# Pair sums in the plain pair, early w2 groups, merged steps and own residual buffers in a token-mixing kernel

## The chip, the cores and the metric

The kernel runs on one core of a Trainium2 chip. The metric is device time in microseconds (us) of one execution. The core has five engines that run beside each other and wait for one another through semaphores: TensorE (PE in the profile; its weight loads stand as PEld), VectorE (DVE), ScalarE (ACT), GpSimd (POOL) and SyncE (SP), which here only issues DMAs. Every engine, and the DMA queue that an engine feeds, works through its own instructions in order.

## The reference

A linear attention block is followed by a token-mixing MLP, all in fp32, for S = 2048 tokens, D = 512 channels and F = 1792 hidden rows:

```
h  = x + A(layernorm(x))                 # linear attention, wqkv, w_phi, wo
n  = layernorm(layernorm(h))             # one from the outer block, one inside the MLP
u  = gelu(einsum("bsd,sf->bdf", n, w1) + b1)
y  = einsum("bdf,fs->bds", u, w2) + b2
out = h + transpose(y)                   # (S, D)
```

The change touches only the MLP: the product with w1 (over the 2048 tokens), the gelu, the product with w2 (over the 1792 hidden rows) and the last addition.

## The kernel before

**Numbers.** An fp32 operand is split into a high part rounded to fp32r and the rest (`split`, line 59: ACT copies the high part, another engine subtracts). A product of two operands is three fp32r matmuls: high by high, high by low, low by high (`mm3`).

**Attention.** It fills the first half of the time and leaves h in `out` and the normalised tokens `HN[t]` (16 tiles of 128 tokens, high and low) in the buffers of the pool `big`. The change does not touch it.

**w1.** The 14 tiles of 128 hidden rows are worked on in seven pairs p = 0 to 6. Pairs 0, 1, 2 and 6 are plain: 16 token tiles by 2 row tiles by 3 matmuls of 512 columns. Pairs 3, 4 and 5 (`SEVEN`) use a scheme with seven products in place of eight on 2 by 2 blocks: a step takes two token tiles, and has 7 products by 3 matmuls of 256 columns, 21 in all (`seven_step`, line 933). The loop over `RUN` counts n = 0 to 29: n = 0 to 5 are the last six steps of plain pair 2, n = 6 to 13 pair 3, n = 14 to 21 pair 4, n = 22 to 29 pair 5. Pair 6 (`fill`, the lines L66 to L68) comes after the loop, with its weights streamed by `stream` (L670 load, L671 high part, L665 low part).

For each step of `RUN` the weights pass through rings of tiles: SP loads a raw tile (`seven_load`, L868, 4 deep), DVE forms the sums that the seven products need (`seven_sum`, L888 and L890), ACT makes the high part (L894, 3 deep), and DVE the low part (`seven_lo`, L912, 3 deep). In iteration n the low part of step n+1 and the sums of step n+3 are written down. The DVE's work is thus in one fixed row: low part, sums, and between them whatever else the loop puts there. What it puts there: `seven_out(p-1)` from i = 1 on, two operations for each n (L950 to L956, the recombination of the previous pair's PSUM banks and its gelu), and the operands of the two "near" pairs 0 and 1.

**Operands of w2.** After the gelu each pair's `U[p]` needs three sums in a tile `tt` (lines 807 to 810 or 824 to 827), and each of the seven operands its high and low part. For the near pairs 0 and 1, `near_ops` puts four subtractions on POOL (L807 to L810), two copies on ACT (L816, L817) and two subtractions on DVE (L818, L819); it is called at i = 2 of pair 3 (n = 8) and of pair 4 (n = 16), and the ACT and DVE parts follow at i = 4, 5 and 7. Both use the one buffer `tt` of the pool `ut`. The other five pairs go through `operands_u` (L824 to L827 and L62), whose results lie in buffers of `big` that pair 6 has finished reading; there the odd pairs have their `tt` in the buffer `h7`.

**w2.** The weights come in 28 groups of two steps (`GRP` = 2): a load of 512 KB on SP (`load_w2`, L1048), three sums on DVE (L854 to L856, through `sums_of`), the high part on ACT (`hi_w2`, L1066), the low part on DVE (`lo_w2`, L1076). The loads of groups 0, 1 and 2 go to the buffers `hold0` to `hold2`, in which the w1 stage keeps the transformed tokens of i = 0, 1 and 2. `STEPS` is 8 pairs of output tiles sp by 7 pairs p. A step (`step`) is seven products: five wide ones, each with a 512-column matmul by the high weights and a 256-column one by the low weights, and two narrow ones of three 256-column matmuls. For p = 0, and for the last two p (three in the last sp), `products` goes product by product, and for the others `step` does all wide matmuls by the high weights, then those by the low ones, then the narrow ones. At an even step count the next group's low part, the second next one's high part and the third next one's sums are written down.

**The end.** For the first seven sp the results go out through a tile `ot` (pool `uo`, one buffer) with accumulating DMAs on POOL's queue. In the last sp the residual h is loaded from `out` (L1185) into the two halves of the same kind of tile, b2 is added (L1186), then the PSUM banks are added in on DVE as their products end (L1188 to L1198), and SP and ACT issue the last stores.

**What sets the order.** Inside a `manual_schedule` block the named engines keep the order in which the code writes their instructions. What stands outside, such as pair 6's fills, `operands_u` and all of SP's loads, is placed by a planner that simulates the time line and may put it between the instructions of such a block. The first three w2 groups are placed by it too, with `issue_after` as a lower bound.

## Time and profile before

| | |
|---|---|
| median of 3 runs | 521.54 us (521.18 to 522.02) |
| profiled execution | 521.74 us, span 520.0 us |
| PE busy | 511.8 us, 98% of the span |
| DVE busy | 445.0 us, 86% |
| ACT, POOL busy | 296.6 us (57%), 245.7 us (47%) |
| granted TensorE clock | 1.000 |

The span runs from the first to the last instruction; about 1.7 us of the execution's time lie around it. "Busy" for PE counts a matmul from its start to a modelled end, and neighbours overlap, so a short wait of PE can hide in a row that looks fully busy; the distance between the starts of two matmuls tells more. In rows of the time line the first number is the start in us from the span's begin, the second the time to the end of the last instruction of the row, then come engine, line of the kernel, operation, tiles (out<-in), shapes and count, and in brackets the idle time of the engine just before, with what ended it.

### The profile page before, as it was taken

How to read it: one execution, taken by the hardware profiler on the slowest of the kernel's cores; microseconds unless marked ns; L12 is line 12 of the kernel's file. 1: busy time of each engine (PE TensorE's matmuls, PEld its weight loads, DVE VectorE, ACT ScalarE, POOL GpSimd, SP SyncE). 2: the span in 40 equal slices, each digit the busy share in tenths (PEclk: the TensorE clock that was granted, in tenths of full speed). 3: DMA queues.
4: the chain of work that ended last, by engine and by line, in shares of the span. 5: the costliest groups of instructions: out<-in, count | busy, mean ns of one | idle time of the engine just before them, and what ended most of it. 6: DMA issues, size and time to landing. Idle time of an engine off the chain costs nothing. (4 is left out here: it accounts for less than half of the span.)

```text
span 520.0 us, 9480 instructions
## 1 busy us (share of the span) xinstructions
PE 511.8 (98%) x3595; PEld 442.1 (85%) x3595; DVE 445.0 (86%) x789; ACT 296.6 (57%) x494; POOL 245.7 (47%) x188
## 2 busy tenths in 40 slices
PE   8999999999999999999999999999999999999996
PEld 8788888887877767887788999998889999999996
DVE  6893999986899998877787679998999888988984
ACT  6998943524246876668976443556654434434430
POOL 2589799885999999875533003000002112211220
PEclk9999999999999999999999999999999999999999
DMA  8744310000131234343413333346125688667653
GB/s 310 271 139 122 82 42 21 1 1 3 42 123 60 103 84 129 112 128 119 151 50 101 97 88 102 87 123 236 62 88 112 165 184 171 139 151 190 139 71 102
DMA packets 36300, 58.56 MB, mean 113 GB/s; under 512 B 3744, under 2 KB 19360, under 8 KB 36256
## 3 DMA queue, kind: packets, MB, share of 16 engines
q1 hardware_dynamic: 31648, 50.85, 30.6%
q0 software_dynamic: 4032, 6.42, 9.8%
q8 instruction: 28, 0.46, 0.4%
q10 hardware_dynamic: 576, 0.69, 0.4%
q14 instruction: 16, 0.13, 0.1%
HBM read 46.81 MB, written 11.14 MB: 111 GB/s over the span
## 5 line engine op out<-in xcount | busy, mean ns | idle before, releaser
L1066 ACT ACTIVATE whi<-wraw 128x1792 fp32r<-128x1792 f32 x28 | 47.6, 1701 | 42.5 <-DVE wraw L856 21.1
L1076 DVE TENSOR_TENSOR wlo<-wraw,whi 128x1792 fp32r<-128x1792 f32 x28 | 56.6, 2020 | 8.8 <-PE py L1108 7.5
L1169 POOL DMA_DIRECT2D out<-ot x7 | 6.2, 885 | 110.4 <-DVE ot L1165 110.4
L67 PE MATMUL pu<-hs,whi 128*128 128x512 f32 x128 | 50.3, 393 | 1.2 <-POOL hs L62 1.2
L1104 PE MATMUL py<-uf,whi 128*128 128x512 f32 x175 | 50.0, 395 | 0.4 <-DVE uf L62 0.4
L66 PE MATMUL pu<-hs,whi 128*128 128x512 f32 x128 | 50.1, 399 | 0.0
L68 PE MATMUL pu<-hs,wlo 128*128 128x512 f32 x128 | 48.3, 390 | 0.0
L894 ACT ACTIVATE whi<-wraw 128x896 fp32r<-128x896 f32 x24 | 22.9, 953 | 33.8 <-DVE wraw L890 18.6
L456 POOL TENSOR_TENSOR ez<-eq,zB 128x1024 f32<-128x1024 f32 x16 | 38.4, 2400 | 4.4 <-ACT zB L503 4.4
L1108 PE MATMUL py<-uf,whi 128*128 128x256 f32 x210 | 39.0, 283 | 0.0
L933 PE MATMUL pu<-ht,whi 128*128 128x256 f32 x192 | 35.6, 283 | 0.0
L208 POOL TENSOR_TENSOR pk<-pk,sk 128x1024 f32<-128x1024 f32 x16 | 30.9, 1940 | 7.3 <-DVE sk L207 7.2
L62 POOL TENSOR_TENSOR hs<-hb,hs 128x512 fp32r<-128x512 f32 x16 | 22.4, 1400 | 23.9 <-ACT hs L61 23.8
L550 ACT ACTIVATE pht<-tn 128x512 f32<-128x512 f32 x32 | 17.4, 595 | 28.4 <-PE tn L548 28.3
L474 POOL TENSOR_TENSOR eq<-eq,w 128x1024 f32<-128x1024 f32 x16 | 32.4, 2027 | 1.3 <-DVE w L471 1.2
L1108 PEld LDWEIGHTS py<-uf,whi 128*128 128x128 f32 x210 | 32.7, 192 | 0.0
L1104 PEld LDWEIGHTS py<-uf,wlo 128*128 128x128 f32 x175 | 28.5, 189 | 4.9
L1104 PEld LDWEIGHTS py<-uf,whi 128*128 128x128 f32 x175 | 29.2, 189 | 3.4 <-DVE uf L62 0.7
L212 POOL TENSOR_TENSOR zacc<-zacc,pk 128x1024 f32<-128x1024 f32 x13 | 31.3, 2405 | 0.5
L66 PEld LDWEIGHTS pu<-hs,whi 128*128 128x128 f32 x128 | 24.0, 188 | 7.1 <-issue 2.5
L933 PEld LDWEIGHTS pu<-ht,whi 128*128 128x128 f32 x192 | 29.9, 192 | 0.0
L912 DVE TENSOR_TENSOR wlo<-wraw,whi 128x896 fp32r<-128x896 f32 x24 | 26.0, 1085 | 4.5 <-ACT whi L894 4.5
(207 smaller groups left out, 1626.9 us busy)
## 6 DMA issues: line engine op xcount, KB each, us to landing
wraw<-in_w SPq DMA_DIRECT2D x28, 512.0 KB, 4.5
wraw<-in_w SPq DMA_DIRECT2D x48, 256.0 KB, 2.8
xraw<-in_xT SPq DMA_DIRECT2D x16, 256.0 KB, 3.1
xh<-in_x SPq DMA_DIRECT2D x16, 256.0 KB, 2.7
h<-in_x SPq DMA_DIRECT2D x16, 256.0 KB, 2.7
out<-h SPq DMA_DIRECT2D x14, 256.0 KB, 2.9
out<-ot POOLq DMA_DIRECT2D x14, 256.0 KB, 4.9
wraw<-in_wT SPq DMA_DIRECT2D x12, 256.0 KB, 4.9
```

Source lines behind the costliest of these rows:

```text
L66: nc.tensor.matmul(o, ah, bh, start=first, stop=False)
L67: nc.tensor.matmul(o, ah, bl, start=False, stop=False)
L68: nc.tensor.matmul(o, al, bh, start=False, stop=last)
L208: nc.gpsimd.tensor_mul(heads(PK[t]), heads(PK[t]), sk.unsqueeze(2).to_broadcast([P, 2 * H, DH]))
L212: nc.gpsimd.tensor_add(zacc, zacc, PK[t])
L456: nc.gpsimd.tensor_mul(EZ[t], EQ[t], zB)
L474: nc.gpsimd.tensor_mul(heads(EQ[t]), heads(EQ[t]), W[t].rearrange("p g c h -> p (g c h)").unsqueeze(2).to_broadcast([P, 2 * H, DH]))
L933: nc.tensor.matmul(ACC[p][bk][:, half], WS[p, i][x][:, a], hb[b][y], start=i == 0 and half == 0 and k == 0, stop=i == NT // 2 - 1 and k == ...
L1066: nc.scalar.activation(WH[g], RAW[g], AF.Copy)
L1076: nc.vector.tensor_sub(wl_, RAW[g], WH[g])
L1104: nc.tensor.matmul(o, w, u, start=p == 0 and not low, stop=p == NP - 1, skip_group_check=True)
L1108: nc.tensor.matmul(bank[bk][:, half], AW[sp, p][x][:, a], UB[p, b][:, y], start=p == 0 and half == 0 and i == 0, stop=p == NP - 1 and i == ...
```

## The change

Five things are done.

1. `near_ops` is called at n = 1 (pair 0) and n = 4 (pair 1), within plain pair 2, and its ACT and DVE parts follow at n = 2, 3, 4 and n = 6, 8, 10. The `tt` of pair 1 goes to the buffer `h7` (`sums_tile`).
2. The helpers for w2's groups stand ahead of the loop. Groups 0 and 1 are loaded at n = 23 and 24 (pair 5, i = 1 and 2), their sums are written at n = 27 and 28, the high part of group 0 at n = 27. The high part of group 1, the low part of group 0 and load and sums of group 2 follow `seven_out` of pair 5, inside the block with written order.
3. In the w2 stage two steps of one group that both go through `step` are merged (`steps`): the wide matmuls by the high weights of both, and then for each of them the rest.
4. In the last sp the residual goes to two buffers of its own, `hb0` and `hb1`.
5. The tile `raw3` is taken for group 4, the first that uses that place, where the code before asked for group 3 and so allocated the place once more.

```diff
--- before.py
+++ after.py
@@ -800,10 +800,13 @@
         nc.scalar.activation(U[f // 2][:, f % 2 * 2:f % 2 * 2 + 2].rearrange("p k d -> p (k d)"), pu,
                              AF.Gelu_apprx_tanh, bias=b1s[:, f:f + 1])
 
+    def sums_tile(p):
+        return h7.tile([P, 3, HD], F32, name="tt", tag="h7") if p % 2 else ut.tile([P, 3, HD], F32, name="tt")
+
     def near_ops(p):
 
         u = U[p]
-        tt = ut.tile([P, 3, HD], F32, name="tt")
+        tt = sums_tile(p)
         nc.gpsimd.tensor_sub(tt[:, 0], u[:, 0], u[:, 1])
         nc.gpsimd.tensor_sub(u[:, 0], u[:, 2], u[:, 0])
         nc.gpsimd.tensor_sub(tt[:, 1], u[:, 2], tt[:, 0])
@@ -820,7 +823,7 @@
 
     def operands_u(p):
         u = U[p]
-        tt = h7.tile([P, 3, HD], F32, name="tt", tag="h7") if p % 2 else ut.tile([P, 3, HD], F32, name="tt")
+        tt = sums_tile(p)
         nc.vector.tensor_sub(tt[:, 0], u[:, 0], u[:, 1])
         nc.vector.tensor_sub(u[:, 0], u[:, 2], u[:, 0])
         nc.vector.tensor_sub(tt[:, 1], u[:, 2], tt[:, 0])
@@ -955,6 +958,51 @@
                 lambda: nc.vector.tensor_add(u[:, 2], acc[2][:, 1], u[:, 2]),
                 lambda: act(1) or nc.vector.tensor_add(u[:, 0], acc[1][:, 1], u[:, 0]) and act(0)]
 
+    STEPS = [(sp, p) for sp in range(NT // 2) for p in range(NP)]
+    NGR = len(STEPS) // GRP
+    RAW, WH, AW = {}, {}, {}
+    done = {"sums": 0, "hi": 0, "lo": 0}
+
+    def load_w2(g):
+        slot = g % 3 if g < 4 else (3, 1, 2, 0)[g % 4]
+        shape = [P, 7, GRP * P]
+        if slot == 3:
+            RAW[g] = raw3 if g == 4 else hp.tile(shape, F32, name="wraw3", bufs=1)
+        else:
+            RAW[g] = hold(shape, F32, "wraw", slot)
+        nc.sync.dma_start(RAW[g][:, 1:5], w2[g])
+
+    def sums_w2():
+
+        g = done["sums"]
+        if g == NGR:
+            return
+        done["sums"] += 1
+        if g not in RAW:
+            load_w2(g)
+        sums_of(RAW[g])
+
+    def hi_w2():
+
+        g = done["hi"]
+        if g == NGR:
+            return
+        done["hi"] += 1
+        WH[g] = keep([P, 7, GRP * P], F32R, "whi", g % 3)
+        nc.scalar.activation(WH[g], RAW[g], AF.Copy)
+
+    def lo_w2():
+
+        g = done["lo"]
+        if g == NGR:
+            return
+        done["lo"] += 1
+        shape = [P, 7, GRP * P]
+        wl_ = hp.tile(shape, F32R, name="wlo1", bufs=1) if g % 2 else keep(shape, F32R, "wlo", 3)
+        nc.vector.tensor_sub(wl_, RAW[g], WH[g])
+        for i, step in enumerate(STEPS[g * GRP:(g + 1) * GRP]):
+            AW[step] = WH[g][:, :, i * P:(i + 1) * P], wl_[:, :, i * P:(i + 1) * P]
+
     six, seven = ([lambda i=i, k=k: t_sums(i, k) for k in range(4)] for i in (6, 7))
     t_hi(4)
     for op in six[:2]:
@@ -976,7 +1024,8 @@
         return [lambda c=c: gelu(2 * p + c, PU[p][c]) for c in range(2)]
 
     early = {0: [*seven, *gelus(0)], 1: [lambda: t_lo(6), lambda: t_hi(7), *gelus(1)], 3: [lambda: t_lo(7)]}
-    todo, heavy, late = [], [], []
+    todo, late = [], []
+    NEAR_AT, LATE_AT = (1, 4), (2, 3, 4, 6, 8, 10)
     for n, (p, i) in enumerate(RUN):
         if n == NT // 2 - AHEAD:
             ms.close()
@@ -991,17 +1040,19 @@
                 op()
         sum_with(*todo[:2])
         todo = todo[2:]
-        if heavy:
-            op = heavy.pop(0)
-            op and op()
         if i == 1 and p > SEVEN[0]:
             todo += seven_out(p - 1)
-        if i == 2 and 0 <= p - SEVEN[0] < NEAR:
-            late = near_ops(p - SEVEN[0])
-        if i == 4 and late:
+        if n in NEAR_AT:
+            late += near_ops(NEAR_AT.index(n))
+        if late and n in LATE_AT:
             late.pop(0)()
-            heavy += [late[0], None, late[1]]
-            late = []
+        at = n - len(RUN)
+        if -7 <= at < -5:
+            load_w2(at + 7)
+        if -3 <= at < -1:
+            sums_w2()
+            if at == -3:
+                hi_w2()
     wst.close()
     hp = ctx.enter_context(tc.tile_pool(name="hp", bufs=1, reuse_waits="tile"))
     wst = ExitStack()
@@ -1020,6 +1071,9 @@
     flush()
     for op in seven_out(SEVEN[-1]):
         op()
+    hi_w2()
+    lo_w2()
+    sums_w2()
     ms.close()
     while FN[NP - 1] < NT:
         if FN[NP - 1] % 2 == 0:
@@ -1033,58 +1087,6 @@
     wst.close()
     uo = ctx.enter_context(tc.tile_pool(name="uo", bufs=2, reuse_waits="tile"))
 
-    STEPS = [(sp, p) for sp in range(NT // 2) for p in range(NP)]
-    NGR = len(STEPS) // GRP
-    RAW, WH, AW = {}, {}, {}
-    done = {"sums": 0, "hi": 0, "lo": 0}
-
-    def load_w2(g):
-        slot = g % 3 if g < 4 else (3, 1, 2, 0)[g % 4]
-        shape = [P, 7, GRP * P]
-        if slot == 3:
-            RAW[g] = raw3 if g == 3 else hp.tile(shape, F32, name="wraw3", bufs=1)
-        else:
-            RAW[g] = hold(shape, F32, "wraw", slot)
-        nc.sync.dma_start(RAW[g][:, 1:5], w2[g])
-
-    def sums_w2():
-
-        g = done["sums"]
-        if g == NGR:
-            return
-        done["sums"] += 1
-        load_w2(g)
-        sums_of(RAW[g])
-
-    def hi_w2():
-
-        g = done["hi"]
-        if g == NGR:
-            return
-        done["hi"] += 1
-        WH[g] = keep([P, 7, GRP * P], F32R, "whi", g % 3)
-        nc.scalar.activation(WH[g], RAW[g], AF.Copy)
-
-    def lo_w2():
-
-        g = done["lo"]
-        if g == NGR:
-            return
-        done["lo"] += 1
-        shape = [P, 7, GRP * P]
-        wl_ = hp.tile(shape, F32R, name="wlo1", bufs=1) if g % 2 else keep(shape, F32R, "wlo", 3)
-        nc.vector.tensor_sub(wl_, RAW[g], WH[g])
-        for i, step in enumerate(STEPS[g * GRP:(g + 1) * GRP]):
-            AW[step] = WH[g][:, :, i * P:(i + 1) * P], wl_[:, :, i * P:(i + 1) * P]
-
-    for i in range(3):
-        with tc.issue_after(LO[-9]), tc.issue_after(LD[(-6, -5, -4)[i]]):
-            sums_w2()
-            if i < 2:
-                hi_w2()
-            if i < 1:
-                lo_w2()
-
     PROD = ((2, 1, 0, None), (5, 5, 1, None), (0, 0, 2, 0), (1, 4, 2, 1), (3, 6, 3, None), (6, 2, 4, None),
             (4, 3, 5, None))
 
@@ -1108,14 +1110,18 @@
             nc.tensor.matmul(bank[bk][:, half], AW[sp, p][x][:, a], UB[p, b][:, y], start=p == 0 and half == 0 and i == 0,
                              stop=p == NP - 1 and i == 2, skip_group_check=True)
 
-    def step(sp, p, order):
-        for low in range(2):
+    def steps(sp, ps, order):
+        for p in ps:
             for a, b, bk, half in order:
                 if half is None:
-                    wide(sp, p, a, b, bk, low)
-        for a, b, bk, half in order:
-            if half is not None:
-                narrow(sp, p, a, b, bk, half)
+                    wide(sp, p, a, b, bk, 0)
+        for p in ps:
+            for a, b, bk, half in order:
+                if half is None:
+                    wide(sp, p, a, b, bk, 1)
+            for a, b, bk, half in order:
+                if half is not None:
+                    narrow(sp, p, a, b, bk, half)
 
     def flat(a):
         return a.rearrange("p k d -> p (k d)")
@@ -1141,7 +1147,8 @@
             products(sp, [p], order)
             continue
         if p < NP - run_on:
-            step(sp, p, order)
+            if n % GRP == 0 or p == 1:
+                steps(sp, range(p, min(p + GRP - n % GRP, NP - run_on)), order)
             continue
         if p < NP - 1:
             continue
@@ -1179,8 +1186,7 @@
                 sums_w2()
             continue
 
-        ot = uo.tile([P, 2, 2, HD], F32, name="ot", bufs=1)
-        hb = [ot[:, i] for i in range(2)]
+        hb = [uo.tile([P, 2, HD], F32, name=f"hb{i}", bufs=1) for i in range(2)]
         for i in range(2):
             nc.sync.dma_start(flat(hb[i]), out[(t + i) * P:(t + i + 1) * P, :])
             nc.vector.tensor_scalar(hb[i], hb[i], b2s[:, t + i:t + i + 1], None, op0=ALU.add)
```

## The prediction

> **What bounds the kernel now.** I read the page first, then the waits of PE and its weight loads, then the busy times by stretch, and last the time line at each place where PE loses time.
>
> ```profile
> span 520.0 us, 9480 instructions
> PE 511.8 (98%) x3595; PEld 442.1 (85%) x3595; DVE 445.0 (86%) x789; ACT 296.6 (57%) x494; POOL 245.7 (47%) x188
> ```
> ```profile
> PEld pu L933 <- DVE wlo L912: 1.3, 4, 0.5
> ```
> PE bounds the kernel, and the change removes no matmul. So it can win only waits of PE, and the time after PE's last matmul. In the stages that it touches, PE waits four times in the loop over the seven-product pairs (L933), and once in the w2 stage, which part 2 shows. Here are the four, to be read by the distances between starts:
>
> ```profile
> 329.63 0.40 PE L933 MATMUL pu<-hs,whi 128*128 128x256 f32 x2
> ...
> 329.99 0.40 PE L933 MATMUL pu<-hs,whi 128*128 128x256 f32 x2
> ...
> 330.84 0.41 PE L933 MATMUL pu<-ht,whi 128*128 128x256 f32 x2
> ```
> ```profile
> 332.99 0.40 PE L933 MATMUL pu<-hs,whi 128*128 128x256 f32 x2
> ...
> 333.58 0.28 PE L933 MATMUL pu<-ht,whi 128*128 128x256 f32 x1
> ```
> ```profile
> 335.74 0.40 PE L933 MATMUL pu<-hs,whi 128*128 128x256 f32 x2
> ...
> 336.65 0.28 PE L933 MATMUL pu<-ht,whi 128*128 128x256 f32 x1
> ```
> ```profile
> 338.80 0.40 PE L933 MATMUL pu<-hs,whi 128*128 128x256 f32 x2
> ...
> 339.40 0.28 PE L933 MATMUL pu<-ht,whi 128*128 128x256 f32 x1
> ```
> Three undisturbed matmuls take 0.36 us (329.63 to 329.99). The four disturbed threes take 0.85, 0.59, 0.91 and 0.60, so 0.49 + 0.23 + 0.55 + 0.24 = 1.51 us are lost. Each time PE waits for the low part of the weights, made by DVE. Busy time by stretch (PE, PEld, DVE, ACT, POOL) shows why:
>
> ```profile
> 280.00:290.00 10.00, 10.00 (x46) 8.29 (x45) 6.28 (x13) 4.02 (x7) 1.33 (x2) 1.00 0.27 80
> ```
> ```profile
> 312.00:333.00 21.00, 20.78 (x174) 20.57 (x173) 20.74 (x42) 10.27 (x13) 4.68 (x4) 1.00 0.36 101
> 333.00:354.00 21.00, 20.71 (x169) 20.15 (x168) 18.82 (x42) 10.22 (x15) 0.00 (x0) 1.00 0.46 138
> 354.00:380.00 26.00, 26.00 (x124) 21.67 (x123) 25.68 (x52) 16.89 (x28) 0.00 (x0) 1.00 0.39 132
> ```
> In pair 4 (312 to 333) DVE is busy for 20.74 of 21 us: here it falls behind. In the plain pair (280 to 290) it has 3.7 of 10 us free, and ACT 6.0.
>
> **Part 1: the near pairs' sums move into the plain pair.** What stands in DVE's row in pair 4 and goes:
>
> ```profile
> 313.85 0.96 DVE L888 TENSOR_TENSOR wraw<-wraw 128x256 f32<-128x256 f32 x1
> 314.84 1.46 DVE L890 TENSOR_TENSOR wraw<-wraw 128x128 f32<-128x128 f32 x2
> ...
> 317.23 0.96 DVE L888 TENSOR_TENSOR wraw<-wraw 128x256 f32<-128x256 f32 x1
> 318.22 0.62 DVE L890 TENSOR_TENSOR wraw<-wraw 128x128 f32<-128x128 f32 x2
> ...
> 319.76 0.42 DVE L888 TENSOR_TENSOR wraw<-wraw 128x256 f32<-128x256 f32 x1
> ```
> ```profile
> 328.34 1.22 DVE L818 TENSOR_TENSOR un<-u,un 128x1024 fp32r<-128x1024 f32 x1
> ...
> 334.42 0.95 DVE L819 TENSOR_TENSOR un<-tt,un 128x768 fp32r<-128x768 f32 x1
> ```
> While POOL does pair 1's four subtractions (its 4.68 us, x4, in the stretch 312 to 333), DVE's sums are stretched: L888 twice from 0.42 to 0.96, L890 once from 0.62 to 1.46, together 1.92 us. L818 takes 1.22 more, right ahead of the first wait at 330. So DVE gets 3.1 us before 330.62, and 0.95 (L819) after that. PE was held up by 0.55 at most at one place, so I count all four waits as gone: **-1.51 us**. Bounds: if the planner fills the freed time with the sums of pairs 2 and 3 ahead of the low parts, the gain is 0; more than 1.51 isn't there. I take 1.51, since the relief is several times the largest wait.
>
> The Trainium skill says in "SBUF — State Buffer", section "Who interferes with whom", that a VectorE instruction with two SBUF inputs and a GpSimd one that reads SBUF exclude each other for a whole instruction. The trace agrees in kind, not in size: 4.68 us of POOL cost DVE 1.92. By the rule DVE could lose all 4.68 wherever these subtractions stand; then the relief here is larger, the gain the same 1.51, and the new place is dearer (rival 4).
>
> At the new place everything issued counts: four POOL subtractions, two ACT copies, two DVE subtractions for each pair. POOL has nothing else there (1.33 us of 10), so nothing queues behind them. ACT's copies come behind the high part of step n+3. DVE's first subtraction (n = 3) waits for ACT's first copy, and the low part of step 5 queues behind it. DVE then has 1.22 + 0.95 for pair 0 and again up to 1.92 of stretching for pair 1, 4.1 us against the 3.7 free in these 10 us, and the code keeps the low parts a step ahead of PE: cost 0; 0.4 without that step, 4.1 without the free time too. Pair 1's two DVE subtractions (n = 8, 10) fall in pair 3, where pair 0's stood, so nothing changes there. `h7` is free once `t_lo(7)` (n = 3) has read it.
>
> **Part 2: w2's first two groups.** From DVE's row, w1's last low part, and later a w2 group's low part, the first of its sums, and pair 6's last operands:
>
> ```profile
> 348.97 1.07 DVE L912 TENSOR_TENSOR wlo<-wraw,whi 128x896 fp32r<-128x896 f32 x1
> ...
> 386.63 2.02 DVE L1076 TENSOR_TENSOR wlo<-wraw,whi 128x1792 fp32r<-128x1792 f32 x1
> 388.56 0.68 DVE L854 TENSOR_TENSOR wraw<-wraw 128x512 f32<-128x512 f32 x1
> 389.17 1.02 DVE L62 TENSOR_TENSOR uf<-tt,uf 128x512 fp32r<-128x512 f32 x2
> ```
> A group's sums are one L854 (0.68) and two more sums of L888's shape (0.42): 1.5 us, twice 3.0, out of the saturated stretch 354 to 380 and into n = 27 and 28. There no sums of w1 are left (step 29's are done at n = 26), which frees 0.42 + 0.62 a step. Behind group 0's sums on DVE queues step 29's low part: it ended at 350.04, and PE needs it in its last step, which starts 2.52 (21 by 0.12) before the fills at 354.15, at 351.63. That is 1.6 us for an insertion of 1.5, without the relief of part 1: cost 0; without that cover, 1.5. On ACT the high part of group 0 goes ahead of pair 6's first high parts; ACT has half of 333 to 354 free: 0. On SP the two loads pass the last two loads of w1 and three of pair 6's; they wait for PE's steps n = 22 and 23 (`hold0`, `hold1`), about when those wait for DVE: 0, and the rival below prices it. The later part (high 1, low 0, load and sums 2) stands where the planner had put much the same: 0.
>
> What it brings is less clear, at the one wait of the w2 stage:
>
> ```profile
> 389.12 0.40 PE L1104 MATMUL py<-uf,whi 128*128 128x512 f32 x1
> 389.90 0.50 PE L1104 MATMUL py<-uf,whi 128*128 128x512 f32 x1 [0.39 <-DVE uf L62]
> ```
> Pair 6's last operands (389.17) come behind a low part and a sum, and PE takes 0.78 from start to start where 0.23 is usual (part 3's row: five in 1.32, the last of them 0.40, so 0.92 for four), 0.55 us lost. With 3.0 us less to do before, DVE lets pair 6's fills or the near products go ahead sooner, and either takes the low part out of that queue: **-0.55**. Ends: -0.55, and +1.0 if PE takes near products first and has less left while it waits (rival 3). I take the first, by the saturated row.
>
> **Part 3: merged steps.** Ten times two steps change the order of the same 32 matmuls.
>
> ```profile
> 383.47 1.32 PE L1104 MATMUL py<-uf,whi 128*128 128x512 f32 x5
> ...
> 385.95 0.63 PE L1104 MATMUL py<-uf,whi 128*128 128x512 f32 x2
> ```
> A step takes 2.48 us, from its first wide matmul to the next step's (385.95); the five wide ones are spaced 0.23. In a merged step the low parts are wanted five of these (1.2 us) later, but PE doesn't wait for them here, and the second step's high parts are wanted 1.3 us sooner. **0**, between -0.1 and +0.1 (a border of lengths could cost 0.01, 20 of them). Part 5 (`raw3`) moves nothing: 0.
>
> **Part 4: residual buffers.**
>
> ```profile
> 508.42 0.80 SPq L1185 DMA_DIRECT2D ot<-out  x2
> ...
> 512.24 0.48 DVE L1186 TENSOR_SCALAR ot<-ot,b2s 128x512 f32<-128x512 f32 x1 [0.52 <-DMA ot<-out]
> 512.83 0.42 DVE L1188 TENSOR_TENSOR ot<-py,ot 128x256 f32<-128x256 f32 x1
> ...
> 516.13 0.74 DVE L1198 TENSOR_TENSOR ot<-py,ot 128x256 f32<-128x256 f32 x2
> ```
> ```profile
> 510.16 0.38 ACT L1187 ACTIVATE e<-py 128x256 f32<-128x256 f32 x1 [6.14 <-PE py L1108]
> ```
> ```profile
> 515.24 0.28 PE L1108 MATMUL py<-uf,wlo 128*128 128x256 f32 x1
> ```
> The residual is loaded at 508.42, when the previous `ot` has been stored, and DVE starts its ten operations at 512.83, though bank 0 was whole at 510.16. They then run back to back, and the second L1198 starts at about 516.54. With own buffers the loads wait for no store. DVE can follow the banks, which end every 1.08 us (9 by 0.12), and the last add starts when PE ends (515.52, plus the 0.04 that ACT needed at 510.16): 515.56. **-0.98**; 0 if the planner still issues the loads late, and no more, since PE then is the end.
>
> **Sum.** -1.51 - 0.55 + 0 - 0.98 = -3.0 against this execution's own 521.74 us (span 520.0 and 1.7 around it): 518.7. The median of the runs is 0.2 lower; I leave that for small new waits of the size seen at 332.99 (0.23). Forecast **518.7 us**.
>
> **The rivals.**
>
> 1. *The four waits stay.* The planner already put sums of pairs 2 and 3 between DVE's row here; it may fill the freed time again. For it speaks DVE's 20.74 of 21; against it, that pair 2's sums can now be done in pair 3, as `ut` is free sooner. Then the end alone is won, perhaps the wait at 389: 520.2 to 520.8.
>
> 2. *The moved loads slow w1's last two.* Loads by size, and their time to landing:
>
> ```profile
> wraw<-in_w SPq DMA_DIRECT2D x28, 512.0 KB, 4.5
> wraw<-in_w SPq DMA_DIRECT2D x48, 256.0 KB, 2.8
> wlo<-in_w SPq DMA_DIRECT2D x8, 256.0 KB, 4.1
> ```
> Alone a load of 256 KB takes 2.8 us; pair 6's, issued among w2's of 512 KB, take 4.1. So w1's last two could land 1.3 late each, and DVE's row is held behind their sums. Without any lead that is 1.3 to 2.6 of wait: 520.0 to 521.3. Against it: raw tiles are loaded four steps (10 us) ahead. The Trainium skill ("DMA: Bandwidth & Descriptors", section "Issuing engines are not separate DMA queues") says that all transfers run on the same 16 DMA engines and interleave; the 4.1 agrees.
>
> 3. *Slower: PE takes w2's first steps ahead of pair 6.* Their operands are ready sooner, and the planner may put them before the fills. Pair 6's gelu, sums and operands then come late, and PE has nothing to do meanwhile. In this trace PE had products until 389.12 for operands that came at 389.9. Each step put ahead of the fills takes 2.48 us of that cover. Two more steps ahead cost 5 us: 521.7 - 1.5 - 1.0 + 5 = 524.2. It decides from 3.5 us on (a step and a half). Against it: the far operands wait for buffers that the fills free.
>
> 4. *POOL holds DVE in the plain pair.* If each of pair 1's subtractions keeps DVE for its whole length, DVE loses 4.68 us and has 2.17 us of pair 0's besides, 3.2 more than it has free from 280 to 290; without the step that it is ahead, PE waits so long: 521.9. Against it stands the 1.92 measured for the same four. By the skill's lock, named above, this is the case.
>
> **How the numbers follow.** Forecast case (518.0 to 519.4) 0.59; rival 1, whole or in part, 0.20; rival 2 0.07; rival 3, or another new wait of its size, 0.09; rival 4 0.05. Range **517.9 to 521.0**: the first case, most of rivals 1 and 2. Some 0.2% (1 us) is what can be told from no change; with it: faster 0.81 (forecast, rival 1, a little of 2), same 0.10 (rivals 2 and 4, the rest of 1), slower 0.09 (rival 3).
>
> **What would show it.** Part 1: both L818 before 300 us, the second L807 before 292, no L888 at 0.96 in pair 4, no wait of L933 for L912. Part 2: L1048 first among the last L868, L854 before the fills; L1104's wait for L62 gone. Part 3: step distances of 2.48 as before. Part 4: L1186 ahead of 510, and the last L1198 within 0.1 us of PE's end. The prediction is wrong if waits for L912 appear at new places in the loop, above all in the plain pair or at n = 28, if the fills start late, or if the wait at 389 grows.

## The result, and the profile after

The changed kernel takes 517.93 us (median of 4 runs, 517.88 to 518.56), beside 521.60 us for the kernel before (4 runs, 521.18 to 522.02). The ratio is 0.9932, with a 95% interval of 0.9915 to 0.9950: 3.7 us faster. The profiled execution took 518.56 us. From the page of the changed kernel, the span, the busy times and the engines' shares of the chain that ended last:

```profile
span 516.8 us, 9476 instructions
...
PE 510.9 (99%) x3595; PEld 442.9 (86%) x3595; DVE 445.5 (86%) x789; ACT 296.8 (57%) x494; POOL 245.0 (47%) x188
```
```profile
PE 89%; POOL 7%; DVE 2%; ACT 1%; issue 1%; POOLq 0%
```
The busy times are those of before within 1 us: nothing became cheaper, only waits went. The list of PE's waits (engine, line that waits, releaser, total us, count, longest) has three rows left, none of them in w1's seven-product loop or in w2:

```profile
PE pu L67 <- POOL hs L62: 1.2, 1, 1.2
PE pk_ps L301 <- DVE eps L57: 1.1, 1, 1.1
PE pk_ps L137 <- ACT wkh L293: 0.2, 1, 0.2
```
The busy times by stretch (PE, PEld, DVE, ACT, POOL) answer to those shown of before:

```profile
280.00:290.00 10.00, 10.00 (x46) 8.29 (x45) 7.87 (x12) 5.65 (x8) 5.66 (x6) 1.00 0.20 53
312.00:333.00 21.00, 21.00 (x177) 21.00 (x177) 18.69 (x44) 9.14 (x11) 0.00 (x0) 1.00 0.38 107
333.00:354.00 21.00, 21.00 (x173) 20.87 (x173) 18.37 (x40) 11.98 (x16) 0.00 (x0) 1.00 0.57 184
```
DVE has 2.3 us free in pair 4, where it had 0.3. POOL's subtractions now stand in the plain pair, where DVE went from 6.28 to 7.87.

A busy row hides short waits, so I measure the kernels by the starts of certain PE matmuls: "seven" is the time from the first to the last matmul of `seven_step`; "sp 0" from there to the 98th matmul of w2 by count, which is pair 6's last fills, the near products and the first groups; "w2" from there to PE's last matmul; "end" from that start to the end of the span. The work in each is the same in all kernels. The run times stand in the last columns, with the median of the kernel before on the same chip.

| kernel | seven | sp 0 | w2 | end | us (before) | ratio, 95% |
|---|---|---|---|---|---|---|
| before | 61.83 | 37.53 | 123.68 | 4.73 | | |
| after | 60.35 | 36.84 | 123.46 | 3.50 | 517.93 (521.60) | 0.9932 [0.9915, 0.9950] |
| part 1 alone | 60.35 | 37.51 | 123.64 | 3.69 | 519.81 (521.19) | 0.9973 [0.9963, 0.9983] |
| part 2 alone | 62.95 | 36.83 | 123.68 | 4.31 | 520.91 (521.19) | 0.9995 [0.9984, 1.0007] |
| part 3 alone | 61.84 | 37.51 | 123.50 | 4.09 | 521.19 (521.19) | 0.9999 [0.9990, 1.0008] |
| part 4 alone | 61.83 | 37.51 | 123.64 | 3.49 | 520.33 (521.19) | 0.9986 [0.9977, 0.9996] |
| all but part 1 | 62.67 | 36.81 | 123.46 | 3.49 | 520.31 (521.34) | 0.9980 [0.9971, 0.9990] |
| only `tt` in `h7` | 60.35 | 37.53 | 123.64 | 3.81 | 519.36 (521.34) | 0.9965 [0.9951, 0.9980] |
| that, and parts 2 to 4 | 60.35 | 36.81 | 123.46 | 3.50 | 518.38 (521.38) | 0.9943 [0.9928, 0.9957] |
| subtractions on DVE | 61.93 | 38.61 | 123.89 | 4.75 | 523.03 (521.38) | 1.0027 [1.0016, 1.0038] |
| `tt` buffers exchanged | 60.88 | 37.15 | 123.88 | 4.42 | 520.50 (521.30) | 0.9989 [0.9978, 0.9999] |
| part 2, loads written later | 62.17 | 36.84 | 123.68 | 3.52 | 521.34 (521.38) | 0.9998 [0.9988, 1.0007] |
| after, w2 sums earlier | 61.69 | 36.78 | 123.72 | 3.50 | 519.55 (521.34) | 0.9967 [0.9954, 0.9980] |
| after, longer merges | 60.35 | 36.97 | 126.49 | 3.50 | 521.44 (521.34) | 1.0000 [0.9991, 1.0010] |

From before to after the four columns fall by 1.48, 0.69, 0.22 and 1.23 us, 3.62 together. The spans differ by less, 3.18, because in this execution of the changed kernel PE lost 0.47 us more in the first 10 us of the span; no line of the change is there, and this start scatters by 1.1 us over the kernels of the table. The medians differ by 3.67.

### The profile page after: what moved, and what is told of

Its sections match the earlier page's. It is cut to its first block, busy times and chain, and to the rows that moved or that the text cites. A ratio compares the mean times of both kernels' runs of the same rounds, so it can differ in the third digit from the quotient of the medians.

```text
span 516.8 us, 9476 instructions
## 1 busy us (share of the span) xinstructions
PE 510.9 (99%) x3595; PEld 442.9 (86%) x3595; DVE 445.5 (86%) x789; ACT 296.8 (57%) x494; POOL 245.0 (47%) x188
## 4 chain that ended last, share of the span: by engine, by line
PE 89%; POOL 7%; DVE 2%; ACT 1%; issue 1%; POOLq 0%
PE py L1106 17%; PE pu L936 12%; PE py L1110 10%; PE pu L66 7%; PE pu L67 7%; PE pu L68 7%; PE pv L67 3%; PE pv L68 3%; PE pv L66 3%; PE pk_ps L66 2%; PE pk_ps L68 2%; PE pk_ps L67 2%; POOL ez L456 2%; POOL eq L474 2%; PE po L68 2%; PE tn L548 2%
## 5 line engine op out<-in xcount | busy, mean ns | idle before, releaser
L1002 DVE TENSOR_TENSOR wlo<-wraw,whi 128x1792 fp32r<-128x1792 f32 x28 | 56.6, 2021 | 8.4 <-PE py L1110 6.9
L1106 PE MATMUL py<-uf,whi 128*128 128x512 f32 x175 | 48.4, 393 | 0.0
L62 POOL TENSOR_TENSOR hs<-hb,hs 128x512 fp32r<-128x512 f32 x16 | 22.4, 1400 | 23.9 <-ACT hs L61 23.8
L1110 PE MATMUL py<-uf,wlo 128*128 128x256 f32 x105 | 29.7, 283 | 0.0
```

The source lines that it names most:

```text
L1002: nc.vector.tensor_sub(wl_, RAW[g], WH[g])
L1106: nc.tensor.matmul(o, w, u, start=p == 0 and not low, stop=p == NP - 1, skip_group_check=True)
L1110: nc.tensor.matmul(bank[bk][:, half], AW[sp, p][x][:, a], UB[p, b][:, y], start=p == 0 and half == 0 and i == 0, stop=p == NP - 1 and i == ...
```

## The experiments

### Each part alone

The diffs are those of the front of this document, one part at a time: `near_ops` and `sums_tile`; the w2 helpers with the loop's loads and sums, and with them part 5 (`raw3`); `steps`; the tiles `hb0` and `hb1`.

> Part 1 alone (the near pairs' sums in the plain pair, pair 1's tt in h7), the rest as before. Theory: DVE's overload in pair 4 is the whole cause of the four waits of L933 for L912, so all four go, 1.5 us; the wait of the w2 stage for L62 (0.55 us) stays, as DVE between 354 and 380 us has the same work; about 520.0 us. Rival A: the planner fills the freed time with the sums of pairs 2 and 3 and the four waits stay, at most 0.3 us gained. Rival B: the w2 stage's wait goes too, since the sums of pairs 2 and 3 are done earlier: 519.4 us.

> Part 2 alone (w2's groups 0 and 1 loaded and summed in pair 5), the near pairs' sums where they were before. Theory: the w2 stage's waits (0.55 to 0.7 us) go, and the four waits of L933 stay or grow, since 3.0 us of sums come behind a DVE that is already late; the sums at n = 27 and 28 stand where no sums of w1 are left, so at most 0.5 us of new wait at the last step: 520.9 to 521.5 us. Rival: without part 1 the insertion of 1.5 us ahead of the last low part isn't covered, and PE waits up to 1.5 us at the last step: 522 us or more.

> Part 3 alone (merged steps). Two readings. From the changed kernel's trace, in which the distance from w2 matmul 97 to the last is 0.2 us shorter: the sixth to tenth 512-column matmul in a row start 0.227 us apart, the first five 0.233, so ten merges give some 0.2 us, and the waits stay as before: 521.3 us. Rival, the prediction's: 0, between -0.1 and +0.1; then the 0.2 us come from elsewhere.

> Part 4 alone (residual buffers of their own). Theory: L1186's two operations run long before bank 0 is whole, the last add starts 0.04 us after PE's last matmul ends, 0.98 us are gained on DVE, and 0.2 more because the last store no longer leaves within 0.7 us of the two others: 520.4 us, all waits of PE as before. Rival: the store's part is scatter of one execution, then 0.98 alone.

Part 1 alone takes all four waits away (61.83 to 60.35) and leaves the wait of the w2 stage. Part 2 alone takes that one away (37.53 to 36.83), but PE then waits longer in the seven-product loop. These are the weight loads' waits there, of part 2 alone, and DVE's row with what it waited for:

```profile
PEld pu L933 <- DVE wlo L912: 2.3, 6, 0.8
```
```profile
347.64 0.42 DVE L888 TENSOR_TENSOR wraw<-wraw 128x256 f32<-128x256 f32 x1 [0.72 <-DMA wraw<-in_w]
```
By PE's starts the two new waits are 0.33 at 349.8 and 0.82 at 352.7 us, 1.15 together, more than the 0.7 gained. The single parts sum to 1.38 + 0.28 + 0 + 0.86 = 2.52 us by their medians; all together give 3.67. Of the missing 1.15 us some 0.3 is not in the kernels' work: the runs of part 1 alone have 2.1 us of their time outside the span, those of the kernel before on the same chip 1.8; why, no run shows. The other 0.8 is, to within what these times can tell (some 0.5 us each), the price that part 2 pays only when it is alone. The next kernel tests that.

### All but part 1

```diff
-        if n in NEAR_AT:
-            late += near_ops(NEAR_AT.index(n))
+        if i == 2 and 0 <= p - SEVEN[0] < NEAR:
+            late = near_ops(p - SEVEN[0])
...
-        tt = sums_tile(p)
+        tt = ut.tile([P, 3, HD], F32, name="tt")
```


> The changed kernel without part 1: near pairs' sums back in pairs 3 and 4, one tt, parts 2, 3 and 4 kept. Theory (parts add up): 1.5 us lost, the four waits of L933 back at their places, 519.4 us. Rival: part 2's sums in pair 5 need part 1's relief, the last low parts come late, and the loss is 2 us or more: 520 us or more.

The four waits come back, and one of 0.81 at 352.4 comes with them: 62.67 in place of 60.35. So part 1 is worth 2.32 us here, and 1.48 on the kernel before. The difference is cover for part 2.

### What part 1 consists of: the buffer, the place, the stretching

First only pair 1's `tt` in `h7`, with every instruction of `near_ops` written where it was; then the same with parts 2, 3 and 4.

```diff
     def near_ops(p):
 
         u = U[p]
-        tt = ut.tile([P, 3, HD], F32, name="tt")
+        tt = sums_tile(p)
```


> Of part 1 only the buffer: pair 1's tt goes to h7, everything else as before, so that POOL's four subtractions of pair 1 need not wait for L819 of pair 0 and leave pair 4. L818 and L819 of pair 1 stay in pairs 4 and 5. Theory: the stretched sums (1.92 us) alone made DVE late enough, since the four waits add up to 1.5 us, so all or nearly all of the 1.5 us go. Rival: the two subtractions, which stand right ahead of the waits at 330.6 and 335.9, cause them, and at least 0.8 us of waits stay.

> The changed kernel with only the buffer of part 1 (pair 1's tt in h7): the near pairs' operations stand where they were before, parts 2, 3 and 4 are kept. Theory, formed after the run with the buffer alone, in which all four waits went: POOL's place is what counts, and the move of L818 and L819 isn't needed for them. Whether it is needed as cover for part 2 is open. If it isn't: no wait of L933, same time as the changed kernel, 517.9 us. Rival: L819 of pair 1 and part 2's sums together are too much for pair 5, and 0.3 to 1.1 us of waits come back at the last two steps, 518.2 to 519 us.

This one line does all of it: 60.35, no wait of PE in the loop. With the other parts the stages are those of the changed kernel to 0.03 us, and the ratios' intervals overlap. The new iterations for the ACT and DVE parts bring nothing that can be measured in time. They do leave a lead: with them w1's last low part ends 0.5 us before PE's last step starts, with the one line and parts 2 to 4 just as it starts. From the time line of the kernel with the one line alone, POOL, then DVE:

```profile
283.98 0.79 POOL L810 TENSOR_TENSOR tt<-u 128x256 f32<-128x256 f32 x1 [2.56 <-PE pu L67]
```
```profile
313.85 0.42 DVE L891 TENSOR_TENSOR wraw<-wraw 128x256 f32<-128x256 f32 x1
314.19 0.42 DVE L827 TENSOR_TENSOR tt<-u 128x256 f32<-128x256 f32 x1
...
327.38 1.22 DVE L821 TENSOR_TENSOR un<-u,un 128x1024 fp32r<-128x1024 f32 x1
328.52 1.08 DVE L915 TENSOR_TENSOR wlo<-wraw,whi 128x896 fp32r<-128x896 f32 x1
...
333.37 1.08 DVE L915 TENSOR_TENSOR wlo<-wraw,whi 128x896 fp32r<-128x896 f32 x1
```
Two things follow from the buffer. POOL's subtractions for pair 1 no longer wait for pair 0's `tt` to come free at 313, so they run at 284 and stretch nothing in pair 4 (the sum at 313.85 takes 0.42, not 0.96). And `ut` is free before pair 1 is done with its own `tt`, so the planner puts pair 2's four sums (L827 to L830) at 314 to 317, where before they ran after L819. In turn pair 3's four sums, which use `h7` too, now wait for pair 1 and start at 334.70. In the kernel before, by the buffers that they wait for pair 3's sums started at 330.81 and pair 2's at 336.63, both among the low parts that PE waited for (the first and third of the four late ones are shown):

```profile
329.48 1.08 DVE L912 TENSOR_TENSOR wlo<-wraw,whi 128x896 fp32r<-128x896 f32 x1
...
330.81 0.42 DVE L824 TENSOR_TENSOR tt<-u 128x256 f32<-128x256 f32 x1
...
335.29 1.08 DVE L912 TENSOR_TENSOR wlo<-wraw,whi 128x896 fp32r<-128x896 f32 x1
...
336.63 0.42 DVE L824 TENSOR_TENSOR tt<-u 128x256 f32<-128x256 f32 x1
...
339.38 0.42 DVE L827 TENSOR_TENSOR tt<-u,tt 128x256 f32<-128x256 f32 x1
```
L821, the 1.22 us subtraction of pair 1 (L818 before), is still in its old place and costs nothing.

The starts of the four late low parts show which of the two counts here; the loop starts at 292.20 in both traces. Before they are 329.48, 332.22, 335.29 and 338.04, with the one line 328.52, 330.51, 333.37 and 336.12, so they come 0.96, 1.71, 1.92 and 1.92 us sooner. PE's waits, added up to each of them, were 0.49, 0.72, 1.27 and 1.51 us, so each relief is enough. From the third on the relief is the 1.92 us of the stretching: pair 2's sums stand ahead of these low parts as well, only at another place in the row, and at the first one they take back half of it. So in this kernel the stretching is what went, though it stood 12 to 16 us ahead of the first wait; DVE's row lists no idle time in between.

Two more runs take one of the two without the other. The first takes the stretching away without the buffer: on the kernel before, pair 1's subtractions go to DVE.

```diff
+        eng = nc.vector if p else nc.gpsimd
-        nc.gpsimd.tensor_sub(tt[:, 0], u[:, 0], u[:, 1])
+        eng.tensor_sub(tt[:, 0], u[:, 0], u[:, 1])
...
```


> The kernel before with pair 1's four subtractions on VectorE in place of POOL, at the same place in pair 4. Theory: POOL stretches DVE's sums by 1.92 us there; without POOL that goes and four times 0.33 = 1.34 us come, so DVE is relieved by 0.6 us, L888 stays at 0.42, and the four waits fall from 1.5 to about 0.9 us: 520.9 us. Rival: the waits depend on L818's and L819's place and not on DVE's sum of work, then they stay at 1.5 us; or they grow, if the stretching cost less than 1.34.

DVE's row in pair 4:

```profile
313.76 0.42 DVE L889 TENSOR_TENSOR wraw<-wraw 128x256 f32<-128x256 f32 x1
...
318.68 0.42 DVE L951 TENSOR_TENSOR u<-pu,u 128x256 f32<-128x256 f32 x1 [0.53 <-ACT u L942]
...
321.35 1.08 DVE L913 TENSOR_TENSOR wlo<-wraw,whi 128x896 fp32r<-128x896 f32 x1
```
The stretching is gone, and the low part still starts at 321.35, as it did before at 321.34. The 1.92 us won went into an in-order wait for ACT at 318.68 (0.53) and into the four subtractions themselves (1.6 us, to 321.35). The four waits stayed, and "sp 0" lost 1.1 us more, most of it in a longer wait of PE for pair 6's operands (L62: 1.2 us in the list of PE's waits, 0.4 before). This run showed no gain from less stretching, but it could not: it put as much work in as it took out. The second run takes pair 2's sums out and keeps the stretching, on the kernel before: pair 2's sums get `h7` and pair 3's `ut`, and POOL stays where it was.

```diff
     def operands_u(p):
         u = U[p]
-        tt = h7.tile([P, 3, HD], F32, name="tt", tag="h7") if p % 2 else ut.tile([P, 3, HD], F32, name="tt")
+        tt = ut.tile([P, 3, HD], F32, name="tt") if p % 2 else h7.tile([P, 3, HD], F32, name="tt", tag="h7")
```


> The kernel before with one line changed: in `operands_u` the even pairs take `tt` in `h7` and the odd ones in `ut`, the other way round. The near pairs keep the one buffer of `ut`, and POOL still subtracts for pair 1 in pair 4 and stretches the same sums by 1.9 us. So pair 2's sums no longer wait for L819 of pair 1 (334.4), and pair 3's wait for it instead. If what kept TensorE waiting is only that pair 2's sums come late: they move from 336.6 to about 314 to 317, three or four of the four waits (1.51 us) go, and the time is about 0.3% below the kernel before. If it needs both, POOL out of pair 4 and pair 2's sums early: the four waits stay in sum within 0.5 us of 1.5, pair 3's sums now being the late ones (after 334.4), and the time is within 0.15% of before. If POOL's stretching alone is the cause: the waits grow, since pair 2's 1.34 us of sums now come ahead of the first low part that is late (329), by up to 1.3 us, and the time is up to 0.25% above before.

```profile
292.60 0.42 DVE L824 TENSOR_TENSOR tt<-u 128x256 f32<-128x256 f32 x1
...
313.96 0.96 DVE L888 TENSOR_TENSOR wraw<-wraw 128x256 f32<-128x256 f32 x1
314.96 1.46 DVE L890 TENSOR_TENSOR wraw<-wraw 128x128 f32<-128x128 f32 x2
```
```profile
330.11 0.40 PE L933 MATMUL pu<-hs,whi 128*128 128x256 f32 x2
330.74 0.38 PE L933 MATMUL pu<-hs,wlo 128*128 128x256 f32 x1 [0.23 <-DVE wlo L912]
```
Pair 2's sums went even further ahead, to 292.60, and so out of the row. The stretching is there as before, and only pair 3's sums are left among the late low parts, now behind pair 1's last subtraction (L819) at 335.79. Three of the four waits are gone; the first, 0.50 by the starts, stays. The four low parts start at 329.60, 331.59, 334.45 and 337.20, with the loop's start at 292.32: measured from there they come 0, 0.75, 0.96 and 0.96 us sooner than before.

So what made DVE late was a sum of work. The stretching was worth 1.92 us in the row and pair 2's sums 0.96; the four waits together were 1.51. The stretching covers them all, as the run of the one line shows; pair 2's sums cover the last three, as this run shows; the two do not add up to the gain, since no more than 1.51 could be won. The stretching was never removed with every sum at its old place; that it would be enough by itself is read from the starts. Of the readings on record the first was met in the waits, though not in the time (0.3%); the third could not be, since pair 2's sums went out of the row altogether and not to the place that it assumed. By the starts 1.1 us are won up to PE's last matmul (0.95 and 0.38, less 0.20 in w2), and the spans of all its runs are 1.1 us shorter in the median. The times are only 0.1% below, with an interval that reaches from 0 to 0.2%, since these runs too have 2.1 us outside the span where the others have 1.8.

### Part 2: what made its price, and where the sums have room

Part 2 alone, with both loads written two iterations later, which was meant to put them behind w1's last raw load:

```diff
-        if -7 <= at < -5:
-            load_w2(at + 7)
+        if -5 <= at < -3:
+            load_w2(at + 5)
```


> Part 2 alone as before, but the loads of w2's groups 0 and 1 two steps later (n = 25 and 26), behind w1's last load. In part 2 alone PE lost 1.15 us at two new places, and DVE waited 0.72 us for a raw tile whose load stood behind w2's in SP's queue. Theory: that wait is the smaller part of it, the inserted sums the larger; DVE's wait goes and the new PE waits fall to about 0.5 us. Rival: the sums alone cause it, nothing changes (1.15 us); or the queue alone, and the new waits go. The four older waits stay in each case.

The new waits fall from 1.15 to 0.34 (62.95 to 62.17), and DVE waits for no raw load. But the edit moved nothing. SP's loads are placed by the planner, and it placed them as before: every engine's instructions come in the same order in both traces, and w2's third load is issued 0.43 us ahead of w1's last raw load in both, 48.8 us after the loop's start. Part 2 alone, then with the loads written later:

```profile
341.63 0.34 SPq L970 DMA_DIRECT2D wraw<-in_w  x1
342.06 0.39 SPq L868 DMA_DIRECT2D wraw<-in_w  x1
```
```profile
340.97 0.34 SPq L970 DMA_DIRECT2D wraw<-in_w  x1
341.40 0.39 SPq L868 DMA_DIRECT2D wraw<-in_w  x1
```
So the theory about the loads' place was not tested. What differs is how long the loads took. In the list of DMAs, KB each, then median us from issue to landing, w1's last raw tile before, in part 2 alone, and in the second trace:

```profile
wraw<-in_w SPq DMA_DIRECT2D x1, 256.0 KB, 2.8
```
```profile
wraw<-in_w SPq DMA_DIRECT2D x1, 256.0 KB, 5.6
```
```profile
wraw<-in_w SPq DMA_DIRECT2D x1, 256.0 KB, 4.6
```
A load of 256 KB took up to twice its time beside w2's of 512 KB, and from one execution of the same order to the next it differed by 1 us. Where it took 5.6, DVE idled for 0.72 us and PE lost 0.8 more than where it took 4.6. So part 2's price by itself is not one number: 0.34 us in one execution, 1.15 in the other. The 0.34 is the insertion of the sums: with a subtraction L62 that the planner put between them they hold the last low part up by 2.0 us (348.91 to 350.91), where the prediction had counted 1.5 against a lead of 1.6. In the changed kernel the same thing happens. A raw load is issued right behind a w2 load on SP, and DVE gets it 3.7 us later (335.38 to 339.08):

```profile
334.94 0.34 SPq L973 DMA_DIRECT2D wraw<-in_w  x1
335.38 0.90 SPq L871 DMA_DIRECT2D wraw<-in_w  x2
```
```profile
339.08 0.43 DVE L891 TENSOR_TENSOR wraw<-wraw 128x256 f32<-128x256 f32 x1 [1.40 <-DMA wraw<-in_w]
...
349.04 1.08 DVE L915 TENSOR_TENSOR wlo<-wraw,whi 128x896 fp32r<-128x896 f32 x1
```
DVE idles for 1.40 us, more than in part 2 alone, and PE does not feel it: the last low part ends at 350.1, and PE's last step starts at 350.59 (2.52 before the fills at 353.11). Half a microsecond is what part 1 left over. The next run puts w2's sums three iterations earlier in the changed kernel:

```diff
-        if -3 <= at < -1:
+        if -6 <= at < -4:
             sums_w2()
-            if at == -3:
+            if at == -6:
```


> The changed kernel with the sums of w2's groups 0 and 1 and the high part of group 0 written three steps sooner (n = 24 and 25), a step behind their loads. Theory: what covers part 2 is the place, where the loads have landed and w1 has no sums left; one step (2.5 us) after the load's issue it hasn't landed (4.5 us), DVE stands in order before it and w1's low parts queue behind: two waits of 1 to 3 us each less DVE's lead of some 2.5 us, so 1 to 4 us slower, 519 to 522 us, with L933 waiting for L912 in pair 5. Rival: DVE's lead covers it all, no change.

It has one wait of 1.35 us at 345.0: `seven` is 61.69. The time is as the theory said, but not its reason: DVE waited for no load of w2. At n = 24 and 25 the sums of w1 are still due and a raw load is late (DVE waits 1.23 us for it), and two insertions of 1.5 us each are more than the lead; at n = 27 and 28 there is room.

### Part 3: longer merges

```diff
-            if n % GRP == 0 or p == 1:
-                steps(sp, range(p, min(p + GRP - n % GRP, NP - run_on)), order)
+            first, end = (1, 4 + sp % 2) if p < 4 + sp % 2 else (4, 5)
+            if p == first:
+                steps(sp, range(first, min(end, NP - run_on)), order)
```


> The changed kernel with longer merges: the wide matmuls by the high weights of three steps (even sp) or four (odd sp) in a row. If the sixth and later 512-column matmuls in a row start 0.227 us apart and the first five 0.233, each step more in a row gives 0.02 us: ten more steps in a row, 0.1 to 0.2 us, 517.8 us. Rival: the low parts' buffers come free later, the low part of pairs 5 and 6 is late by up to 0.5 us in some sp, and it is slower: 518 to 521 us.

Merging over groups loses the whole gain of the other parts, 3.0 us in w2. Weight loads' waits of this kernel:

```profile
PEld py L1106 <- DVE ot L1173: 2.4, 3, 0.9
PEld py L1106 <- DVE wlo L1002: 1.0, 4, 0.3
```
DVE waited for PE before low parts (L1002) for 11.5 us in the w2 stage, and for 8.4 in the changed kernel: the longer the run of wide matmuls, the later PE frees the buffers of the low parts. DVE then comes late to the output blocks (L1173), which read the PSUM banks that PE wants next.

## Why the prediction was right, and where it was not

The forecast was 518.7 in a range of 517.9 to 521.0, with 0.81 on faster; it is 517.93, faster. That is 0.03 us inside the lower edge, and so near an edge it is luck to be inside: the changed kernel's own runs scatter by more. By its steps:

**Part 1, -1.51 us: right in size and in mechanism, with two slips.** All four waits went (-1.48), because DVE's row was relieved by more than it was late. Of the step's "relief 1.92, 1.22 and 0.95" the 1.92 of stretching is enough by itself: in the one-line run L818 and L819 stay in place, and it gains as much. The first slip is the yardstick. The step set the relief against the largest wait (0.55), where it must be set against the waits added up, 1.51, and counted ahead of each: in the run with exchanged buffers a relief of 0.96 leaves one wait, since it comes behind the first. The second is a term left out. That `ut` is free sooner stood there only as an argument against rival 1; it takes pair 2's sums out of the row (in the changed kernel they start at 293.65), and the exchange shows that this alone wins about 1.0 of the 1.5. Rival 1's filling came in part: in the changed kernel pair 3's sums stand in this row as before (from 328.63), but with so much relief they cost no wait.

**The new place at cost 0: right.** The stretching moved with POOL into the plain pair (POOL, then DVE):

```profile
284.42 0.79 POOL L810 TENSOR_TENSOR tt<-u 128x256 f32<-128x256 f32 x1 [2.55 <-PE pu L67]
285.28 0.74 POOL L811 TENSOR_TENSOR u<-u 128x256 f32<-128x256 f32 x1
285.98 0.78 POOL L812 TENSOR_TENSOR tt<-u,tt 128x256 f32<-128x256 f32 x1
286.85 1.60 POOL L813 TENSOR_TENSOR tt<-u,tt 128x256 f32<-128x256 f32 x1
```
```profile
284.64 1.53 DVE L893 TENSOR_TENSOR wraw<-wraw 128x128 f32<-128x128 f32 x2
286.12 1.73 DVE L821 TENSOR_TENSOR un<-u,un 128x1024 fp32r<-128x1024 f32 x1
287.77 1.22 DVE L917 TENSOR_TENSOR wlo<-wraw,whi 128x512 fp32r<-128x512 f32 x1
```
Against 0.62, 1.22 and 0.69 undisturbed, that is 1.95 us, as much as the 1.92 in pair 4, and PE did not wait. Rival 4's price was not paid: VectorE lost half of POOL's 3.9 us (the four rows), not all of it. The Trainium skill ("SBUF — State Buffer", section "Who interferes with whom") says that the ports which the two engines share are an exclusive lock and that issue order decides who blocks. Row by row this trace agrees: POOL's third subtraction is done at 286.76, and L821, issued at 286.12, takes 0.51 longer; POOL's fourth is issued at 286.85 while L821 runs until 287.85, and takes 1.60 where the second took 0.74. So a part of POOL's time is its own waiting, and the prediction's "agrees in kind, not in size" set VectorE's loss against the whole of it.

**Part 2, cost 0: right with part 1, and the cover was named, but its working failed.** "1.6 us for an insertion of 1.5, without the relief of part 1: cost 0" was tried by itself and cost 1.15 us in one execution and 0.34 in another of the same order. The step counted 1.5 for an insertion that took 2.0, which is the 0.34, and it set the two loads to 0 on SP, where a late raw load cost the other 0.8. That is rival 2's mechanism, which I gave 0.07 and 1.3 us of delay for each load; the last raw load took 2.8 and 1.8 us longer. In the changed kernel it took 2.9 us longer, and that was hidden.

**The wait at 389, -0.55: went, and -0.69 was won.** I left out the second, small gap behind it (0.11). Rival 3's order did not come: one w2 matmul stands among the first fills, at 354.04 in PE's row, but the next one at 362.43, and 17 of them start ahead of pair 6's last matmul, where it was 26 before. No wait followed.

**Part 3, 0 (-0.1 to +0.1): it gave 0.2.** In PE's row, before and then after, from a step's first wide matmul to the same place two steps on:

```profile
401.46 1.32 PE L1104 MATMUL py<-uf,whi 128*128 128x512 f32 x5
402.62 0.76 PE L1104 MATMUL py<-uf,wlo 128*128 128x256 f32 x5
...
406.41 0.63 PE L1104 MATMUL py<-uf,whi 128*128 128x512 f32 x2
```
```profile
399.67 2.46 PE L1106 MATMUL py<-uf,whi 128*128 128x512 f32 x10
401.96 0.76 PE L1106 MATMUL py<-uf,wlo 128*128 128x256 f32 x5
...
404.60 0.63 PE L1106 MATMUL py<-uf,whi 128*128 128x512 f32 x2
```
4.95 against 4.93, ten times. I had bounded a border by 0.01 for each of 20, and had the sign open; the trace shows what it is (below). Part 3 alone can't be told from nothing by its time.

**Part 4, -0.98: the mechanism was right, the size is one execution's.** The last add starts 0.32 us after the start of PE's last matmul, when that has ended, as the step said; before it was 1.22 (515.24 to 516.46). The step read that last add's start as 516.54, 0.08 too late, so by its own working the term is -0.90.

```profile
505.54 0.88 DVE L1192 TENSOR_SCALAR hb<-hb,b2s 128x512 f32<-128x512 f32 x2
...
513.61 0.42 DVE L1204 TENSOR_TENSOR hb<-py,hb 128x256 f32<-128x256 f32 x1 [0.32 <-PE py L1110]
```
But "end" of the eight kernels of the table with the old tile runs from 3.52 to 4.75 us, while all six with the new buffers stand at 3.49 or 3.50. The execution that I worked from (4.73) was nearly the worst; in three of the eight the last add already starts 0.32 us after PE's last matmul. Part 4 alone gave 0.14%, 0.7 us.

**The sum.** I left the median's 0.2 us for new small waits. There were none, and w2, sp 0 and the end each gave a little more than counted; together that is the distance from 518.7 to 517.9.

## What to carry to other kernels

When an engine in a fixed row comes late, go back along its row to where it last had time to spare, add up what could leave it, and set that against the waits added up: here the stretched sums stood 12 to 16 us ahead of the first wait. Ask too which buffer holds work at its place. One line that gave a temporary tile its own place did the work of a whole rescheduling, because it let POOL's subtractions run 29 us sooner. A cost that is covered by another part's gain is to be priced by itself as well, its loads above all: beside large loads a small one took up to twice its time here, a different time in each execution, and half a microsecond of lead was all that hid it. Before a run's number is explained, its trace should be searched for the edit: the loads that were written later had not moved. And a gain at the end of a kernel that depends on when stores land should be read from several executions.

## What the runs showed of the hardware

A matmul with 512 columns that follows ones with 256 is a little slower at first. In the rows above, five take 1.16 us up to the next row (401.46 to 402.62), and ten take 2.29 (399.67 to 401.96), not 2.32: the first five are 0.232 apart, the later ones 0.227. A run of ten pays the slow start once where two runs of five pay it twice, and ten merges of 0.02 to 0.03 make the 0.2 us. Why it is so, no run shows.

The time from PE's last matmul to the end, with the same instructions there, varied by 1.2 us over the eight kernels with the old tile, and by 0.8 us (4.31 and 3.52) between the two executions of part 2 that have the same order throughout. It goes with the moment at which the residual's loads are issued, 6.8 us before PE's last matmul in the profiled execution of before and 8.0 us in the one with an end of 3.52; that load waits for the store of the block before it (19.4 us in the list of SP's waits of before).
